# Batch 1's loads of x asked for behind the weights instead of behind a gate, with new instruction tables

## The chip, the cores and the metric

The kernel runs on one core of a Trainium2 chip. The metric is the time of one execution on the device in microseconds. Engines: TensorE (PE in the profile, its weight loads PEld), VectorE (DVE), ScalarE (ACT), GpSimd (POOL) and SyncE (SP), which only asks for transfers. Each engine runs its own instructions in the order in which the program lists them; an instruction that waits holds up all that stand behind it on that engine.

## The reference

```python
# x: 4 x 12480 x 128, inducing: 32 x 128, w_in: 128 x 2048, w_out: 2048 x 128, all float32
def mab(q, kv):                       # softmax attention, scale = 1/sqrt(128)
    s = scale * (q @ kv.transpose(0, 2, 1))
    a = np.exp(s - s.max(-1, keepdims=True))
    a /= a.sum(-1, keepdims=True) + 1e-09
    return a @ kv
h = mab(I, x)                         # 32 inducing rows attend to the 12480 rows of a batch
y = mab(x, h)                         # each row attends to the 32 results
t = y @ w_in
g = t * np.clip(t + 3.0, 0.0, 6.0) / 6.0
out = g @ w_out
```

## The kernel before

A batch (0 to 3) goes through two passes. The rows of a batch are cut into seven *groups*: six of 2048 rows (128 partitions of 16 rows, 1024 KB) and a last one of 192 rows. The groups make 25 *chunks* of up to 512 rows.

**Pass 1** of batch b reads each group once: a load of x into an `xr` buffer (`load_x`, L207, from GpSimd's queue; five such buffers), a cast to bfloat16 in four parts (`k`, L357; buffer `xb`, two of them), transposes on TensorE (`T`, L366) that are copied to `xT` (`x`, L375), scores against the inducing rows (`s`, L381), their exponentials (`a`, L393), the aggregation `hnd` (`g`, L419) and a running sum of the weights (`y`, L432). An `xr` buffer is free again when its group's `g` is done.

**Between the passes**, from the 32 aggregated rows: the sum of the weights (`dred`, `den`, `rD`), `H`, its transpose `HT`, the tables `W` and `Wd` (L492, L498), and `dH`. Because the 32 rows are few, the two layers behind the attention are folded into small coefficient tables. `G` (L517) is the first layer applied to the 32 rows; `hs`, `L`, `lt` and `BD` make the linear table; for the quadratic table, 16 blocks are squared (`dp` L616 and `q` L628 to L631 in batch 0) and multiplied with w_out (`C`, L642), which gives `Cq` (L655).

**Pass 2** of batch b goes chunk by chunk: `bp` (L783) and its exponentials `TF` (L796); the small exponentials `dk` (L762, three buffers, one for each group of chunks) are spread over the partitions by a transfer that SyncE asks for (`d<-dk`, `b_spread`, L771, six buffers `d`); `TD` is the product of both (L807); `op` sums the linear part (`b_lin`, L818) and 16 matmuls with Cq (`b_quad`, L837); VectorE scales the result by r_all (L857) into `os`, which SyncE stores. `ep`, `e`, `sp`, `nf`, `rp` and `r` make r_all.

**The order.** Pass 1 of batch 0, the tables of batch 0 and pass 1 of the first group of batch 1 are the *prologue*; its instructions stand in the list ORDER, token by token, and `first` carries them out. After it comes a loop over all 100 chunks, t = 0 to 99. In step t, chunk t is summed, the `bp` of chunk t + 2 computed, its products one step later, and the spread of chunk t + 6 asked for. All else (the rest of pass 1 of batch 1, then pass 1 and the tables of batches 2 and 3) is put into slots of these steps by the list PLAN: `@2.8 k1.2.3:A` means that in step 2, at place 8 among its places 0 to 28, part 3 of group 2 of batch 1 is cast by ScalarE (A; D is VectorE, P is GpSimd). ORDER and PLAN are written by a planner from costs and due times.

The tokens that the change touches: `dx5`, `dx6` and `dx10` in ORDER ask for groups 5 and 6 of batch 0 and group 0 of batch 1; `dwi` and `dwo` ask for w_in (two transfers) and w_out (four); `held` is a gate and four loads: GpSimd copies one element of the spread of chunk 3, so it waits until that has landed, and then asks for groups 1 to 4 of batch 1. `made` is a gate of the same kind that waits for dH. `wl` and `wo` are the eight and four pieces in which the low part of w_in and the bfloat16 copy of w_out are made; `bk`, `bT`, `bx`, `bs`, `ba`, `bg`, `by` are group 0 of batch 1; `warm` are matmuls whose results nobody reads; `half` is four small VectorE instructions (half_rows). BY_DVE names the blocks whose squares VectorE makes instead of ScalarE.

```python
elif kind == "held":
    gate("seen", S[0][("d", 3)][:, 0:1])
    while held:
        load_x(1, held.pop(0))
```

Of the kernel before, what the change touches and what calls it, by code (L numbers as in the profile page):

```python
# [40 lines left out]
k1.3.2:A g1.1.0 g1.1.1 @5.0 T1.4.0 @5.2 k1.5.1:D @5.3 s1.2 a1.2 lx2.0 @5.4 T1.3.1 @5.7 k1.5.3:A @5.12 y1.2
g1.2.0 k1.5.0:D @5.22 T1.3.0 x1.3.0:A x1.3.1:D x1.4.0:D @6.0 g1.2.1 @6.6 k1.5.2:A @6.8 s1.3 T1.5.0 a1.3 y1.3
k1.6:P T1.6.0 x1.6a @6.24 s1.4 a1.4 x1.5.0:D @7.2 y1.4 lx2.1 @7.3 g1.3.0 g1.3.1 @7.5 sp0.3 T1.5.1 g1.4.0
k2.0.0:P k2.0.3:D @7.8 T1.6.1 x1.6 nf0.3 k2.0.2:D x1.5.1:A @7.22 lx2.2 @7.23 s1.5 a1.5 @8.1 k2.2.2:P @8.3
g1.4.1 @8.21 k2.0.1:D @8.28 s1.6 a1.6 y1.5 y1.6 @9.4 k2.2.1:P @9.5 k2.2.0:P @9.8 T2.0.1 @9.12 dred1 @9.20
T2.0.0 @9.21 lx2.3 @9.22 x2.0.1:A @10.2 k2.1.2:A @10.24 x2.0.0:A @10.28 den1 k2.1.3:A @11.4 g1.5.0 da1 @11.24
g1.5.1 g1.6.0 g1.6.1 rD1 H1 @12.4 s2.0 @12.5 lx2.6 htp1 @12.8 HTb1 @12.12 a2.0 HT1 @12.28 pp0.5 ep0.6 dk0.5
pp0.6 ep0.5 e0.5 lx2.4 HTl1 G1.0 G1.1 G1.2 @13.0 e0.6 @13.3 G1.3 Gc1.0 k2.1.0:A @13.7 g2.0.0 @13.20 Gc1.1
k2.2.3:A g2.0.1 @13.21 hs1 dG1.2 k2.1.1:A @13.22 T2.1.1 x2.1.1:D @13.23 dG1.0 @13.24 sp0.4 @13.28 dk0.6 @14.0
nf0.4 @14.2 sq1.2 @14.6 dG1.3 T2.2.1 x2.2.1:A T2.1.0 sq1.0 k2.3.1:D dG1.1 T2.2.0 x2.2.0:A @14.12 x2.1.0:D Wd1  # L50
L1.0 L1.1 @14.21 Lc1 @14.24 sq1.3 @15.3 lx2.5 @15.5 s2.1 a2.1 @15.6 dG1.4 @15.20 sq1.1 dG1.11 @15.22 k2.3.2:P
y2.0 @16.8 k2.4.0:P @16.28 pp1.0 dk1.0 @17.0 ep1.0 g2.1.0 e1.0 @17.7 lt1 @17.8 sq1.4 sp0.5 nf0.5 k2.3.3:A C1.2
dG1.5 @17.21 C1.0 BD1 @17.23 sq1.5 @18.8 sp0.6 dG1.8 k2.4.3:P @18.20 y2.1 sq1.11 dG1.13 @18.21 C1.4 @19.6
g2.1.1 k2.4.2:A @19.12 sq1.8 @19.23 nf0.6 k2.4.1:P @20.0 sp1.0 @20.1 dG1.12 C1.11 C1.5 @20.6 s2.2 a2.2 @20.24
T2.3.1 sq1.13 @20.28 k2.3.0:D T2.3.0 C1.8 nf1.0 @21.2 dG1.9 g2.2.0 x2.3.1:A @21.5 x2.3.0:D @21.7 sq1.12 @21.8
sq1.9 @21.20 dG1.6 @21.23 dG1.14 @22.12 k2.5.0:P W1 @22.21 C1.3 lx3.0 ep1.2 e1.2 pp1.1 ep1.1 dk1.1 e1.1 pp1.2
@23.0 dk1.2 sq1.6 @23.2 T2.4.1 x2.4.1:D @23.3 dG1.7 C1.13 @23.20 sq1.14 @23.21 dG1.10 @24.12 C1.1 sq1.7 C1.12
@24.20 s2.3 a2.3 dG1.15 k2.5.3:A @24.23 k2.5.1:D C1.6 @25.0 k2.5.2:P @25.2 sp1.2 y2.2 C1.14 g2.2.1 T2.4.0
@25.4 C1.7 g2.3.0 sq1.10 T2.5.0 C1.9 sq1.15 g2.3.1 C1.15 @25.5 x2.4.0:A C1.10 nf1.2 lx3.2 T2.5.1 @25.6 s2.4
x2.5.0:A sp1.1 Cq1 @25.12 nf1.1 x2.5.1:A k2.6:P T2.6.1 @25.28 x2.6 @26.3 a2.4 @26.7 s2.5 @26.22 y2.3 @27.0  # L60
g2.4.0 T2.6.0 g2.4.1 @27.3 a2.5 k3.0.3:P @27.5 x2.6a @27.12 y2.4 @27.24 k3.0.1:P @27.28 s2.6 a2.6 pp1.4 dk1.4
pp1.3 ep1.4 e1.4 y2.5 y2.6 dred2 @28.2 ep1.3 e1.3 @28.3 g2.5.0 g2.5.1 g2.6.0 k3.0.0:A @28.4 den2 rD2 k3.0.2:A
dk1.3 @28.8 da2 @28.22 lx3.1 k3.1.0:D g2.6.1 H2 @29.4 lx3.3 @29.5 T3.0.0 @29.24 htp2 HTb2 @30.6 k3.1.3:A
@30.12 k3.1.1:P @30.23 HT2 HTl2 @31.5 x3.0.0:A lx3.4 @31.8 W2 @31.24 lx3.6 @32.3 T3.1.0 G2.0 G2.1 G2.2 G2.3
@32.4 T3.0.1 x3.1.0:A @32.5 Gc2.0 @32.7 x3.0.1:A k3.1.2:A hs2 @32.8 Gc2.1 dG2.2 @32.20 dG2.9 @33.20 sp1.3
@34.4 k3.2.2:P sq2.2 @34.22 T3.1.1 x3.1.1:D nf1.3 @34.23 k3.3.0:P @35.0 s3.0 a3.0 @35.6 k3.3.1:P @35.12 ep1.6
e1.6 dG2.6 ep1.5 pp1.6 pp1.5 e1.5 dk1.5 @35.21 k3.2.0:D @35.24 k3.2.1:P @36.3 y3.0 @36.7 g3.0.0 sq2.6 @36.20
dk1.6 @36.22 g3.0.1 dG2.0 @36.23 k3.2.3:D k3.3.2:A @36.24 sp1.4 T3.2.0 x3.2.0:A @37.1 k3.3.3:P sp1.5 nf1.5
@37.2 L2.0 L2.1 @37.6 sq2.9 nf1.4 @37.20 dG2.1 @37.21 T3.2.1 x3.2.1:D @37.28 sq2.0 @38.12 dG2.4 @38.20
k3.4.0:A @38.21 k3.4.1:D sq2.1 @39.12 lx3.5 @40.0 dG2.5 @40.2 s3.1 a3.1 C2.2 @40.7 C2.1 @40.20 sq2.4 @40.21  # L70
dG2.3 @40.22 s3.2 a3.2 @40.24 sq2.5 dG2.7 @41.2 T3.3.0 @41.6 T3.3.1 @41.12 x3.3.0:A @41.28 C2.5 @42.5 Lc2
@42.6 C2.6 @42.7 y3.1 @42.8 sq2.7 C2.9 @42.12 dG2.10 @42.22 Wd2 @43.2 x3.3.1:D @43.12 sq2.3 dG2.8 @44.0
k3.4.3:P ep2.0 e2.0 pp2.0 dk2.0 pp2.1 ep2.1 g3.1.0 @44.2 C2.4 e2.1 C2.0 @44.3 dk2.1 @44.4 k3.4.2:P @44.6
k3.5.2:D @44.8 sq2.10 @44.20 g3.1.1 @44.21 dG2.15 @44.22 k3.5.3:D lt2 @44.23 T3.4.1 @44.28 sq2.8 @45.1 T3.4.0
x3.4.0:A sq2.15 BD2 @45.5 x3.4.1:D @45.8 dG2.14 C2.3 dG2.11 g3.2.0 @46.6 sp1.6 @46.24 nf1.6 sq2.14 @47.8 sp2.0
nf2.0 @48.2 C2.8 @48.4 sq2.11 dG2.13 pp2.2 @48.5 ep2.2 e2.2 k3.5.0:D @48.8 dk2.2 @49.0 dG2.12 @49.5 k3.5.1:P
@49.21 s3.4 s3.3 @49.22 C2.10 a3.3 @49.23 sq2.13 y3.2 @50.1 T3.5.1 x3.5.1:D C2.7 @50.3 g3.2.1 @50.4 sq2.12
@50.5 k3.6:A C2.14 C2.15 @50.6 C2.12 C2.11 y3.3 sp2.2 T3.5.0 a3.4 sp2.1 C2.13 Cq2 x3.5.0:A g3.3.0 g3.3.1
g3.4.0 nf2.1 s3.5 a3.5 @50.21 y3.4 nf2.2 @51.20 g3.4.1 g3.5.0 T3.6.1 y3.5 @51.24 x3.6 @52.2 T3.6.0 @52.21
x3.6a @53.8 s3.6 a3.6 y3.6 @54.5 g3.5.1 @54.6 dred3 @55.6 g3.6.0 @55.8 den3 rD3 @55.21 da3 @55.22 g3.6.1 @56.0  # L80
pp2.3 dk2.3 @56.2 H3 ep2.5 pp2.5 e2.5 ep2.3 e2.3 @56.6 htp3 @56.28 HT3 HTb3 HTl3 @57.4 G3.0 G3.1 G3.2 G3.3
Gc3.0 Gc3.1 dG3.1 @57.20 dk2.5 @57.28 dG3.0 pp2.4 dk2.4 hs3 ep2.4 @58.1 ep2.6 @58.28 sp2.3 nf2.3 e2.4 sq3.0
@59.0 dG3.4 @60.3 L3.0 sq3.1 L3.1 @60.4 Lc3 @60.5 C3.0 @60.12 dG3.5 sq3.4 Wd3 @60.21 sp2.4 nf2.4 @61.12 e2.6
@61.22 dG3.7 @62.5 sp2.6 @62.6 sq3.5 @62.21 dG3.3 @63.5 sq3.7 @63.12 nf2.6 @63.20 dG3.9 @63.21 sq3.3 @63.24
dG3.2 @64.6 C3.1 @64.21 pp2.6 pp3.0 dk3.0 ep3.0 e3.0 @65.3 sq3.2 @65.4 dG3.6 @65.22 dk2.6 @65.23 C3.7 W3 sq3.9
@66.3 C3.2 @66.4 C3.3 @66.21 sq3.6 @67.2 dG3.10 @67.6 dG3.15 @67.7 sq3.10 @67.20 sp2.5 @67.23 dG3.8 nf2.5
@68.0 C3.6 @68.5 C3.4 sq3.15 @68.21 dG3.13 @69.6 lt3 @69.8 sq3.8 @70.28 dG3.11 @71.2 C3.15 @71.4 C3.10 @71.7
BD3 @71.21 C3.9 @71.28 sq3.13 @72.5 sq3.11 @72.24 dG3.14 @73.0 pp3.1 dk3.1 @73.3 ep3.1 e3.1 @73.4 dG3.12 @73.6
sp3.0 nf3.0 @73.28 sq3.14 @74.12 C3.13 sq3.12 @74.21 C3.8 @74.23 C3.5 @75.0 C3.11 @75.2 C3.14 C3.12 Cq3 @75.6
sp3.1 pp3.2 ep3.2 dk3.2 e3.2 pp3.4 ep3.4 @75.8 dk3.4 @75.24 nf3.1 @76.3 e3.4 @78.24 sp3.4 nf3.4 @79.4 pp3.3  # L90
# [19 lines left out]


# [1219 lines left out]
```

## Time and profile before

| | |
|---|---|
| median of 3 runs | 292.4 us (291.7 to 293.71) |
| the profiled execution's own time | 292.84 us |
| its span, first to last instruction | 291.1 us |
| granted TensorE clock | 0.995 |
| TensorE busy | 282.1 us, 97% |
| moved by DMA | 66.69 MB, mean 229 GB/s |

Times in the profile are microseconds from the start of the span. A row of instructions reads: start, length, engine, line, operation, what is written from what, and count; in brackets, the idle time before it and what ended that. The rows of windows give for each stretch its length and the busy time of each engine. The prologue lasts to about 43, the loop to about 286.

### The profile page before, as it was taken

The page shows a single profiled execution, that of the slowest core. Times are in us where ns is not written, and L with a number is a line of the kernel's source. Part 1 is how long each engine was busy: PE and PEld are TensorE (multiplying, and loading weights), DVE is VectorE, ACT ScalarE, POOL GpSimd, SP SyncE. Part 2 cuts the span into 40 slices and gives each one's busy share as a digit, 9 for nine tenths or more (in the row PEclk, how much of TensorE's full clock was granted, in tenths as well). Part 3 has the DMA queues.
Part 4 walks back from the last instruction along what each step waited for, and adds up shares of the span by engine and source line. Part 5 has one row for each costly group of instructions (what it writes and reads, how often), then busy time and mean ns, then how long its engine had stood idle before and what let it go on. Part 6 is the DMA issues. An engine that isn't in the chain of part 4 may idle for free.

```text
span 291.1 us, 9807 instructions
## 1 busy us (share of the span) xinstructions
PE 282.1 (97%) x3960; PEld 227.6 (78%) x3971; DVE 231.9 (80%) x495; ACT 227.0 (78%) x412; POOL 130.5 (45%) x250
## 2 busy tenths in 40 slices
...
GB/s 258 428 365 270 104 329 402 231 273 281 285 357 161 245 199 177 336 317 259 295 84 216 305 100 148 214 35 203 160 150 182 172 208 222 146 216 217 229 227 156
DMA packets 25137, 66.69 MB, mean 229 GB/s; under 512 B 3168, under 2 KB 18304, under 8 KB 19072
## 3 DMA queue, kind: packets, MB, share of 16 engines
...
q14 instruction: 17, 0.14, 0.2%
...
## 4 chain that ended last, share of the span: by engine, by line
PE 80%; DMA 11%; DVE 5%; issue 1%; ACT 1%; ACTq 0%; DVEq 0%; POOLq 0%
PE op L837 29%; PE bp L783 13%; PE op L818 8%; PE hnd L419 7%; PE pt L366 5%; DMA xr<-in_x_dram 5%; PE cp L642 5%; DMA out_dram<-os 4%; PE s L381 2%; DMA d<-dk 2%; PE sp L687 2%; PE pp L748 2%; PE ep L667 2%; PE lp L585 1%; PE gp L517 1%
## 5 line engine op out<-in xcount | busy, mean ns | idle before, releaser
L796 ACT ACTIVATE TF<-bp 128x512 bf16<-128x512 f32 (+1 forms) x200 | 115.6, 589 | 32.8 <-PE bp L783 18.9
L837 PE MATMUL op<-Cq,TF 128*128 128x128 bf16 (+1 forms) x784 | 100.3, 221 | 0.1
L837 PE MATMUL op<-Cq,TD 128*128 128x128 bf16 (+1 forms) x784 | 98.6, 219 | 0.0
L857 DVE TENSOR_TENSOR os<-op,r_all 128x512 f32<-128x512 f32 x96 | 65.9, 687 | 20.5 <-PE op L837 18.3
L807 DVE TENSOR_TENSOR TD<-TF,d 128x1024 bf16<-128x1024 bf16 (+1 forms) x100 | 74.8, 748 | 0.2
L837 PEld LDWEIGHTS <-TF 128*128 128x128 bf16 (+1 forms) x784 | 56.1, 98 | 21.2 <-issue 11.0
L783 PE MATMUL bp<-xT,W 128*128 128x512 bf16 (+1 forms) x193 | 72.3, 375 | 0.1
L837 PEld LDWEIGHTS <-TD 128*128 128x128 bf16 (+1 forms) x784 | 60.4, 98 | 0.0
L818 PE MATMUL op<-BD,nf 128*128 128x512 f32 (+1 forms) x100 | 54.7, 547 | 0.0
L357 POOL CAST xb<-xr 128x512 bf16<-128x512 f32 x33 | 25.1, 778 | 29.7 <-DMA xr<-in_x_dram 17.5
L544 POOL COPY gate<-TD 128x1 bf16<-128x1 bf16 x48 | 14.1, 294 | 51.2 <-DVE TD L807 49.2
L547 POOL TENSOR_TENSOR dg<-G 128x256 f32<-128x256 f32 x48 | 35.6, 741 | 0.0
L546 POOL TENSOR_TENSOR dg<-G 128x256 f32<-128x256 f32 x48 | 31.5, 656 | 6.9 <-DVE r_all L736 3.6
L554 ACT ACTIVATE sq<-dg 128x512 bf16<-128x512 f32 x48 | 30.0, 629 | 3.8 <-POOL dg L547 2.1
L419 PE MATMUL hnd<-xr,a 128*32 128x128 f32 x384 | 30.6, 227 | 0.0
L366 PE MATMUL pt<-ident_b,xb 128*128 128x128 bf16 x392 | 29.6, 219 | 1.0 <-DVE xb L357 0.5
L419 PEld LDWEIGHTS hnd<-xr,a 128*32 128x32 f32 x384 | 24.8, 109 | 2.7 <-issue 1.3
L366 PEld LDWEIGHTS <-xb 128*128 128x128 bf16 x392 | 23.2, 98 | 4.6 <-issue 1.6
L726 PE MATMUL rp<-one,nf 128*128 128x4 f32 (+1 forms) x100 | 25.6, 257 | 0.9 <-ACT dk L762 0.9
L375 ACT COPY xT<-pt 128x1024 bf16<-128x1024 bf16 (+1 forms) x24 | 22.4, 950 | 2.8 <-PE pt L366 2.6
L642 PE MATMUL cp<-w_out_b,sq 128*128 128x128 bf16 x256 | 22.4, 220 | 0.1
L726 PEld LDWEIGHTS rp<-one,nf 128*128 128x128 f32 (+1 forms) x100 | 18.9, 189 | 3.7 <-ACT dk L762 1.3
...
## 6 DMA issues: line engine op xcount, KB each, us to landing
xr<-in_x_dram POOLq DMA_DIRECT2D x23, 1024.0 KB, 8.1
out_dram<-os SPq DMA_DIRECT2D x23, 1024.0 KB, 4.6
d<-dk SPq DMA_DIRECT2D x96, 128.0 KB, 4.4
os<-in_x_dram SPq DMA_DIRECT2D x1, 1024.0 KB, 5.7
...
w_out_r<-in_moe_w_out_dram POOLq DMA_DIRECT2D x4, 256.0 KB, 10.8
...
xl<-in_x_dram POOLq DMA_DIRECT2D x4, 96.0 KB, 7.0
```

The source lines that it names most:

```text
L366: nc.tensor.transpose(pt[:, (i - lo) * p : (i - lo + 1) * p], xb[:p, i, :], ident_b[:p, :p])
L419: nc.tensor.matmul(st["hnd"][:M, :C], lhsT=st[("a1", g)][:p, i * M : (i + 1) * M], rhs=xs[(b, g)][:p, i, :], start=(g == 0 and i == 0), st ...
L546: nc.gpsimd.tensor_sub(dg[:, 0], stepped(G2, jb, 0, 1, 0), stepped(G2, jb, 2, 0, 2))
L547: nc.gpsimd.tensor_sub(dg[:, 1], stepped(G2, jb, 1, -1, 0), stepped(G2, jb, 10, 0, 2))
L642: nc.tensor.matmul(st["cp"][:, k * C : (k + 1) * C], lhsT=sq[:, k * P : (k + 1) * P], rhs=w_out_b[:, jc, :], start=(k0 == 0 and k == 0), s ...
L726: nc.tensor.matmul(st["rp"][:p, at : at + S_], lhsT=nf[:R, j * p : (j + 1) * p], rhs=one4[:R, :S_], skip_group_check=True,)
L783: nc.tensor.matmul(st[("bp", c, k)][:, :w], lhsT=st["W"][:, k].rearrange("p m i -> p (m i)"), rhs=st[("xT", g)][:, j * w : (j + 1) * w],)
L796: nc.scalar.activation(st[("x", c)][:, k, :w], bp[:, :w], ACT.Exp, scale=scale)
L807: nc.vector.tensor_mul(u[:, :, :w], t[:, :, :w], d[:, :w].unsqueeze(1).to_broadcast([P, 2, w]))
L818: nc.tensor.matmul(op[:p, : S_ * C], lhsT=st[("nf", g)][:R, j * p : (j + 1) * p], rhs=st["BD"][:R, : S_ * C], start=True, stop=False, skip ...
L837: nc.tensor.matmul(op[:p, s * C : (s + 1) * C], lhsT=T[k][:, s * p : (s + 1) * p], rhs=st["Cq"][:, k, :], start=False, stop=(s == S_ - 1 a ...
L857: nc.vector.tensor_mul(ot[:p, j * S_ : (j + 1) * S_, :], op[:p, : S_ * C].rearrange("p (s c) -> p s c", c=C), r_all[:p, b, c, :S_].unsquee ...
```

## The change

The gate and its four loads go out of ORDER. The loads of groups 1 to 4 of batch 1 become tokens `dx11` to `dx14`, which stand behind the weights' loads (`dwo`) on GpSimd, between its first instructions for batch 1. ORDER and PLAN are both computed anew, for x that is there when the loop begins; BY_DVE has one block less. All other code stays. PLAN holds the same tokens as before in other slots and with other engines for some casts and copies; ORDER holds the same tokens but for the loads, the gate, and 11 warming matmuls instead of 14. ORDER now names the engine of a square (`q7:D`), which `first` doesn't read: BY_DVE decides.

```diff
-BY_DVE = (2, 6, 11)
+BY_DVE = (2, 7)
...
 PLAN = """
-@0.0 ep0.2 k1.1.2:P k1.1.1:A k1.1.3:D e0.2 pp0.4 dk0.4 k1.1.0:P pp0.2 k1.2.0:P ep0.4 e0.4 @0.4 k1.2.2:P @0.5
-dk0.2 @0.12 lx1.6 @0.20 sp0.1 nf0.1 @1.22 T1.1.1 x1.1.1:D lx1.5 T1.1.0 @2.0 k1.2.1:P x1.1.0:A @2.8 k1.2.3:A
-@3.2 pp0.3 dk0.3 ep0.3 e0.3 sp0.2 T1.2.0 nf0.2 k1.3.3:P @3.12 T1.2.1 @3.20 k1.3.1:A @3.22 k1.4.3:D k1.4.0:A
+@0.0 k1.2.0:D ep0.4 k1.2.3:P k1.1.1:D k1.2.2:P k1.1.2:P k1.1.3:A e0.4 pp0.2 dk0.2 pp0.4 dk0.4 @0.3 ep0.2 e0.2
+@0.20 sp0.1 nf0.1 @1.2 k1.1.0:P @1.3 k1.2.1:P @1.12 lx1.5 @1.21 T1.2.1 x1.2.1:D @1.22 T1.1.1 x1.1.1:D T1.1.0
+x1.1.0:A T1.2.0 x1.2.0:D @2.0 lx1.6 @2.4 k1.4.0:A @2.8 k1.4.3:D @2.20 ep0.3 e0.3 pp0.3 dk0.3 @3.2 k1.4.2:P
...
 ORDER = """
-k0.0:A k0.2:D k0.1:A warm3:o T0.1:o T0.0:o xT0.1:A xT0.0:D k1.2 warm3:f s0:f a0 k1.0:D k1.1:P
-T1.1:f z1:D z0:A T1.0:f z3:P xT1.1:D z2:A g0.0 xT1.0:D k2.1:P k2.2 g0.1 k2.0:D s1:f dx5 y0
-T2.1:f a1 dx6 T2.0:o xT2.1:D g1.0 g1.1 k3.0:D k3.2 k3.1:D y1 dx10 T3.0:o xT2.0:A dwi warm2:f
-s2:f T3.1:f dwo k4.0:D k4.1:A xT3.0:D a2 T4.0:f xT3.1:D k4.3:A g2.0 k4.2:A xT4.0:D s3:f T4.1:f
-y2 a3 g2.1 xT4.1:A y3 g3.0 g3.1 s4:o k5.0:D k5.1:A k5.3:D k6:A warm2:o T5.0:o k5.2:D a4 T6:f
-T5.1:f xT5.0:D xT6:A g4.0 xT5.1:D s5.0:f g4.1 y4 a5.0 bk2:P s5.1:f bk0:A s6:f g5.0 bk3:P dred
-a5.1 a6 n5.0 bk1:P n5.1 wi0 g5.1 g6 n6 den bT0:o wl0:P rD H wl1:P bx0:A dall warm1:f htp:f bT1:o
-HT Wd HTb bx1:D wi1 warm1:f pe1:ff HTl dH bs:f dk1 wl4:P pe0:fo W ba wo1:P dp13:o e1 dp6:f by
-bg0 made wl7:P e0 q6 bg1 dk0 wo3:P dp5:f q13 sp0:f wl2:P spread0 dp15:f q5 dp2:f nf0 C6 wl3:P
-C13 q15 q2 dp4:o wo0:P G0:o q4 C5 dp1:f dp0:f C15 q1 wl5:D held bp0.0:f wl6:D dp11:o q0 G1 q11
-G2 TF0.0 C4 wo2:A G3 dp8:f C1 hs dp9:f q8 C0 dp14:f q9 bp0.1:f C11 C8 TF0.1 dp12:o cmax dp3:f C9
-q12 half L0:f q14 L1 q3 dp10:f C2 L dp7:o TD0 q10 lt:o C3 q7 C12 BD C10 C14 C7 bp1.1:f rp0:f Cq
-rp1 bp1.0:f TF1.1 TF1.0 warm2:f r0
+k0.2:D k0.0:D warm4:o T0.1:o k0.1:D xT0.1:A T0.0:o xT0.0:D k1.2 warm3:f s0:f k1.1:D k1.0:P z2:D
+z1:A T1.1:f z0:P a0 T1.0:f xT1.1:D z3:A g0.0 xT1.0:D k2.2 g0.1 k2.0:D s1:f dx5 k2.1:D T2.1:f y0
+a1 dx6 T2.0:o xT2.1:D g1.0 y1 g1.1 k3.2 k3.0:D dx10 k3.1:D xT2.0:A warm1:o T3.1:o dwi T3.0:f
+xT3.1:D s2:f k4.2:A k4.3:D dwo xT3.0:D k4.1:A warm2:f T4.1:f k4.0:D a2 s3:f xT4.1:D T4.0:f a3 y2
+g2.0 xT4.0:A g2.1 y3 g3.0 s4:o g3.1 k5.0:D k5.1:A k6:D dx11 k5.2:A k5.3:D warm1:o T5.0:o a4 T6:f
+T5.1:f xT5.0:D xT6:A g4.0 xT5.1:D s5.0:f g4.1 y4 a5.0 bk3:P s6:f bk2:A s5.1:f g5.0 dx12 dred
+a5.1 n5.0 a6 bk1:A bk0:P g5.1 wi0 half n5.1 dx13 n6 den g6 bT1:o wi1 rD H wl1:D htp:f bT0:o HTb
+HT dx14 bx1:A Wd bx0:D pe1:ff HTl dH bs:f dk1 pe0:fo ba dall W made wo2:P dp7:o e1 dp6:f bg0
+q7:D wo1:P q6:A bg1 wo0:P dk0 dp9:f dp0:f wl3:P by spread0 dp2:f q9:A C7 wl0:P dp8:o q0:A C6
+q2:D C9 q8:A wl2:P dp10:o C0 e0 dp5:f wl5:P C8 q10:A bp0.0:f wl4:D dp15:o G0:f q5:A wl7:D G1
+wl6:P TF0.0 dp11:f C2 wo3:P q15:A dp14:o C10 q11:A G2 G3 q14:A dp12:f dp3:f hs bp0.1:o q12:A C15
+C11 TF0.1 C14 dp1:f q3:A C5 cmax L0:o q1:A dp4:f TD0 L1 q4:A dp13:o sp0:f L q13:A C1 lt:f nf0
+C12 C4 BD C3 C13 bp1.0:f bp1.1:f Cq TF1.0 rp0:o rp1 TF1.1 r0
 """.split()
...
             elif kind == "dx":
-                load_x(*((1, 0) if i == 10 else (0, i)))
+                load_x(i // 10, i % 10)
```

More of the change, by code (lines that the diff above doesn't have):

```diff
@@ L31 @@
 SUMG = 5
-BY_DVE = (2, 6, 11)
+BY_DVE = (2, 7)
 SPLIT = (4, 5)
 PLAN = """
-@0.0 ep0.2 k1.1.2:P k1.1.1:A k1.1.3:D e0.2 pp0.4 dk0.4 k1.1.0:P pp0.2 k1.2.0:P ep0.4 e0.4 @0.4 k1.2.2:P @0.5
-dk0.2 @0.12 lx1.6 @0.20 sp0.1 nf0.1 @1.22 T1.1.1 x1.1.1:D lx1.5 T1.1.0 @2.0 k1.2.1:P x1.1.0:A @2.8 k1.2.3:A
-@3.2 pp0.3 dk0.3 ep0.3 e0.3 sp0.2 T1.2.0 nf0.2 k1.3.3:P @3.12 T1.2.1 @3.20 k1.3.1:A @3.22 k1.4.3:D k1.4.0:A
-@4.2 x1.2.1:D s1.1 @4.3 k1.4.2:P a1.1 k1.3.0:A @4.4 T1.4.1 x1.4.1:D @4.5 x1.2.0:D @4.6 k1.4.1:A @4.24 y1.1
@@ L41 @@
[L41 to L90, printed above, removed]
@@ L91 @@
-dk3.3 ep3.3 @79.28 e3.3 @80.6 sp3.2 nf3.2 @82.3 sp3.3 @83.5 nf3.3 @85.4 ep3.5 e3.5 ep3.6 e3.6 pp3.5 pp3.6
-@86.6 dk3.6 @87.8 sp3.5 nf3.5 @88.24 sp3.6 @89.0 dk3.5 @93.5 nf3.6
+@0.0 k1.2.0:D ep0.4 k1.2.3:P k1.1.1:D k1.2.2:P k1.1.2:P k1.1.3:A e0.4 pp0.2 dk0.2 pp0.4 dk0.4 @0.3 ep0.2 e0.2
+@0.20 sp0.1 nf0.1 @1.2 k1.1.0:P @1.3 k1.2.1:P @1.12 lx1.5 @1.21 T1.2.1 x1.2.1:D @1.22 T1.1.1 x1.1.1:D T1.1.0
+x1.1.0:A T1.2.0 x1.2.0:D @2.0 lx1.6 @2.4 k1.4.0:A @2.8 k1.4.3:D @2.20 ep0.3 e0.3 pp0.3 dk0.3 @3.2 k1.4.2:P
@@ new lines @@
+@3.3 s1.1 @3.5 k1.3.3:D @3.8 k1.3.0:D a1.1 @3.20 k1.4.1:P T1.4.0 @3.23 x1.4.0:D T1.4.1 s1.2 @3.24 x1.4.1:A
+@4.0 a1.2 @4.1 k1.3.1:P @4.4 k1.5.0:P @4.6 g1.1.0 T1.3.0 x1.3.0:A g1.1.1 g1.2.0 @4.20 k1.3.2:P T1.3.1 @4.28
+k1.5.1:D y1.1 y1.2 @5.3 s1.4 a1.4 k1.6:P @5.6 sp0.2 @5.22 g1.2.1 x1.3.1:D @5.23 k1.5.3:A @5.28 T1.6.1 @6.3
+lx2.0 @6.4 nf0.2 k1.5.2:A @6.5 s1.3 a1.3 y1.3 @6.8 T1.5.0 x1.5.0:A @6.21 x1.6 @6.24 g1.3.0 @7.0 g1.3.1 sp0.3
+@7.2 T1.6.0 T1.5.1 @7.4 nf0.3 g1.4.0 g1.4.1 @7.6 x1.6a lx2.2 k2.0.2:P s1.6 @7.12 lx2.1 x1.5.1:A @7.21 k2.0.3:D
@@ new lines @@
+@7.23 k2.0.1:P @7.24 k2.0.0:A @8.6 k2.1.0:P @8.8 y1.4 s1.5 a1.5 lx2.4 @8.21 T2.0.1 k2.1.1:P T2.0.0 a1.6
+x2.0.1:A @8.24 k2.2.2:A @8.28 y1.5 @9.0 y1.6 k2.1.2:P @9.2 g1.5.0 x2.0.0:A @9.8 dred1 @10.8 g1.5.1 @10.12
+lx2.3 den1 rD1 @10.20 k2.2.0:A k2.2.1:A @10.21 g1.6.0 g1.6.1 da1 @10.28 H1 s2.0 a2.0 @11.8 htp1 HT1 Wd1 @11.20
+HTb1 @12.0 W1 HTl1 @12.28 pp0.5 dk0.5 ep0.5 ep0.6 e0.6 k2.1.3:D pp0.6 dk0.6 e0.5 k2.2.3:A @13.0 G1.0 G1.1 G1.2
+G1.3 Gc1.0 Gc1.1 @13.2 hs1 @13.24 lx2.6 T2.1.1 x2.1.1:A @13.28 sp0.4 dG1.0 @14.5 T2.2.0 x2.2.0:A @14.6 dG1.2
@@ new lines @@
+@14.8 y2.0 @14.21 sq1.0 dG1.3 g2.0.0 nf0.4 @15.3 T2.1.0 x2.1.0:D k2.3.3:A @15.5 L1.0 @15.7 sq1.2 @15.12 g2.0.1
+sq1.3 @15.20 dG1.1 T2.2.1 x2.2.1:D @15.22 L1.1 Lc1 @16.0 dG1.4 @16.3 C1.0 k2.3.2:A @16.4 lx2.5 k2.4.0:P s2.1
+sq1.1 k2.4.1:D a2.1 @16.5 sq1.4 dG1.11 @16.6 lt1 @16.8 BD1 @16.12 k2.4.2:P @17.2 y2.1 @17.23 C1.3 @17.28 ep1.0
+e1.0 @18.2 pp1.0 dk1.0 dG1.8 k2.3.1:P g2.1.0 @18.3 sp0.5 @18.6 sp1.0 @18.8 nf0.5 @18.12 nf1.0 sq1.11 @18.21
+s2.2 @18.28 k2.3.0:A dG1.5 @19.0 C1.4 @19.3 a2.2 @19.4 sq1.8 @19.6 C1.2 @19.21 g2.1.1 @19.22 sp0.6 nf0.6
@@ new lines @@
+@19.23 sq1.5 @20.1 dG1.12 dG1.9 @20.3 lx3.0 @20.4 C1.8 @20.12 sq1.12 @20.21 dG1.13 T2.3.1 x2.3.1:D @21.3 sq1.9
+@21.7 T2.3.0 x2.3.0:D @21.12 k2.5.0:A @21.21 dG1.6 @21.23 C1.9 sq1.13 @22.2 y2.2 k2.4.3:P dG1.14 @22.21 pp1.2
+dk1.2 pp1.1 dk1.1 ep1.2 e1.2 ep1.1 C1.1 @22.24 e1.1 @23.0 C1.11 sq1.6 @23.8 sq1.14 dG1.7 T2.4.1 x2.4.1:D
+@23.12 C1.5 @23.24 k2.5.3:D dG1.10 @24.2 sq1.7 @24.8 k2.5.1:A @24.20 s2.3 dG1.15 g2.2.0 C1.7 @24.21 a2.3 C1.13
+@24.22 sp1.2 C1.6 C1.12 @24.23 T2.4.0 g2.2.1 @25.0 nf1.2 C1.14 @25.1 g2.3.0 T2.5.0 lx3.2 sq1.10 C1.10 sq1.15
@@ new lines @@
+C1.15 x2.5.0:A @25.2 k2.6:P T2.6.0 @25.3 x2.4.0:D s2.4 a2.4 @25.4 x2.6a Cq1 @25.5 k2.5.2:P @25.6 T2.5.1 g2.3.1
+@25.12 y2.3 y2.4 k3.0.2:D @25.24 x2.5.1:A @25.28 sp1.1 nf1.1 @26.22 g2.4.0 g2.4.1 @26.23 s2.5 @26.28 k3.0.0:A
+a2.5 @27.0 T2.6.1 x2.6 @27.20 y2.5 @27.24 k3.0.1:P @27.28 s2.6 a2.6 lx3.1 g2.5.0 y2.6 dred2 k3.0.3:A @28.0
+ep1.3 e1.3 @28.3 pp1.3 pp1.4 dk1.4 ep1.4 e1.4 dk1.3 g2.5.1 @28.4 k3.1.0:A @28.12 k3.1.3:D @28.20 den2 rD2
+g2.6.0 g2.6.1 @28.23 da2 @29.0 H2 @29.2 T3.0.1 @29.28 htp2 x3.0.1:D @30.4 k3.1.1:A HTb2 HT2 HTl2 @30.12 W2
```

28 lines of the change are left out of this document (added).

## The prediction

> **What bounds the kernel now.** I read the head of the page and the chain by engine first, to see which engine is the limit, then the busy time by stage, to see where that engine rests.
>
> ```profile
> span 291.1 us, 9807 instructions
> PE 282.1 (97%) x3960; PEld 227.6 (78%) x3971; DVE 231.9 (80%) x495; ACT 227.0 (78%) x412; POOL 130.5 (45%) x250
> PE 80%; DMA 11%; DVE 5%; issue 1%; ACT 1%; ACTq 0%; DVEq 0%; POOLq 0%
> ```
> ```profile
> core 0: us, PE busy (x) PEld busy (x) DVE busy (x) ACT busy (x) POOL busy (x), PEclk, DMA share, GB/s
> 0.00:44.00 44.00, 40.73 (x578) 29.47 (x585) 30.74 (x64) 32.91 (x58) 25.75 (x62) 1.00 0.94 293
> 44.00:285.00 241.00, 239.90 (x3371) 197.15 (x3374) 199.28 (x422) 194.04 (x356) 104.71 (x188) 1.00 0.68 220
> 285.00:291.00 6.00, 1.49 (x19) 1.00 (x16) 1.86 (x11) 0.00 (x0) 0.00 (x0) 0.77 0.34 118
> ```
>
> TensorE is busy for 97% of the span and carries 80% of the chain. The loop (44 to 285) leaves it idle for 1.10 us of 241. The change issues the same matmuls in the loop, so whatever it does for x can bring back about 1.1 us there at most. The 3.27 us of idle time before 44 is the only other place, and 4.5 us at the end are the last stores, which the change doesn't touch.
>
> Where is the loop's one idle stretch? The chain in order of time, then TensorE's own row:
>
> ```profile
> 43.50 6.29 DMA d<-dk
> ...
> 51.37 0.61 ACT dk L762
> 52.02 0.27 PE rp L726
> ```
> ```profile
> 52.02 0.27 PE L726 MATMUL rp<-one,nf 128*128 128x4 f32 x1 [0.86 <-ACT dk L762]
> ```
>
> A broadcast of d asked for at 43.50 lands late. It reads a dk buffer, there are three of these, and ScalarE can't write the next dk until it has landed; TensorE waits 0.86 us behind that. A late d is unusual, so I looked at what else the DMA engines carried (columns: window, length, TensorE busy, clock, DMA share, GB/s), and at single transfers in two of the windows (KB each, median us to landing):
>
> ```profile
> 25.00:31.00 6.00, 5.98 (x91) 1.00 1.11 156
> 31.00:37.00 6.00, 5.75 (x93) 1.00 0.56 134
> 37.00:43.30 6.30, 6.30 (x79) 1.00 0.97 349
> 43.30:50.00 6.70, 6.70 (x85) 1.00 1.09 404
> ```
> ```profile
> d<-dk SPq DMA_DIRECT2D x6, 128.0 KB, 2.8
> ```
> ```profile
> q0 software_dynamic: 292, 2.18, 96.0%
> q1 hardware_dynamic: 9, 0.01, 0.9%
> xr<-in_x_dram POOLq DMA_DIRECT2D x3, 1024.0 KB, 9.5
> d<-dk SPq DMA_DIRECT2D x1, 128.0 KB, 7.2
> ```
>
> From 31 to 37 the engines move 134 GB/s and six d take 2.8 us each. From 37 to 50 four loads of batch 1 fill them (349 and 404 GB/s), and a d takes 7.2. These loads start there because of the gate:
>
> ```profile
> 20.55 0.81 POOL L246 DMA_DIRECT2D w_out_r<-in_moe_w_out_dram  x1 [1.75 <-DMA xr<-in_x_dram]
> ...
> 33.05 0.60 POOL L259 CAST w_out_b<-w_out_r 128x512 bf16<-128x512 f32 x1
> 35.93 0.19 POOL L873 COPY seen<-d 128x1 bf16<-128x1 bf16 x1 [2.28 <-DMA d<-dk]
> 36.17 2.20 POOL L207 DMA_DIRECT2D xr<-in_x_dram  x4
> 41.42 1.18 POOL L357 CAST xb<-xr 128x512 bf16<-128x512 f32 x2 [3.04 <-DMA xr<-in_x_dram]
> ```
>
> So the trade of the change is plain: the four loads leave the window of the loop's d (37 to 50) and enter that of the first six d (31 to 37).
>
> **The change, part by part.** The sum is made against the profiled execution's own time, 292.84 us (span 291.1, 1.74 around it), which is 0.44 above the median of the three runs.
>
> *The gate goes, the loads come earlier.* The gate's copy (0.19) and its wait (2.28) leave GpSimd, where only these loads stood behind it: nothing on the path. The four issues cost 2.20 us of GpSimd as before. Now they stand behind the last w_out_r issue (20.55). That issue itself waited 1.75 us, for a load asked for eight GpSimd transfers earlier: with this, each of the four can go only when the transfer eight before it has landed, and when the aggregation has released its x buffer. The loads eight before are the tail of x, batch 1's group 0 and the two halves of w_in; the fourth thus goes at about 27, and GpSimd has nothing to do for a table until dH is there (below), so this wait holds up nobody for long. Data flows behind the weights:
>
> ```profile
> DMA to landing us min/median/max: 9.1/10.8/10.9
> ```
>
> This is w_out_r; 20.55 + 9.1 gives 29.7. Four times 1024 KB are 4.19 MB, at 404 GB/s 10.4 us: x is there at about 40 with nothing else in the way, at about 42 with the six d in between (0.79 MB more). Before, the fourth was asked for at 38, and the last three took 9.5 us in the median: 47. So "there when the loop begins" holds within a few us.
>
> *What it buys.* At 43.5 the loads are over; the d of that time takes 2.8 us instead of 7.2, and the wait of 0.86 goes. What is late next there? The row of the loop leaves 1.10 - 0.86 = 0.24 us of idle time: nothing that a profile can name. Bounds: 0 (the new table waits elsewhere) to 1.1. I take **-0.86**.
>
> *What it may cost: the first six d.*
>
> ```profile
> 31.15 18.47 SPq L771 DMA_DIRECT2D d<-dk  x10
> ...
> 39.87 9.75 SPq L771 DMA_DIRECT2D d<-dk  x4
> ```
> ```profile
> 28.62 0.42 DVE L505 TENSOR_TENSOR dH<-HT 128x256 bf16<-128x256 f32 x1
> ...
> 31.84 0.68 DVE L697 CUSTOM_DVE_ANT_0 nf<-e,sp 128x512 fp32r<-128x512 f32 x1
> ...
> 36.06 0.69 DVE L570 TENSOR_SCALAR r<-gp 128x512 f32<-128x512 f32 x1
> ...
> 38.96 0.28 DVE L596 TENSOR_SCALAR L<-lp 32x128 f32<-32x128 f32 x1 [0.26 <-PE lp L585]
> 39.17 0.67 DVE L807 TENSOR_TENSOR TD<-TF,d 128x1024 bf16<-128x1024 bf16 x1
> 40.05 0.69 DVE L606 TENSOR_TENSOR BD<-lt,one_f 128x512 fp32r<-128x512 f32 x1 [0.21 <-PE lt L601]
> 41.27 0.56 DVE L655 TENSOR_SCALAR Cq<-cp 128x384 bf16<-128x384 f32 x1 [0.53 <-PE cp L642]
> ```
>
> The first d is asked for at 31.15. With the loads beside it I give it the 7.2 us of the one d that stood behind them: 38.4 instead of 34. The new ORDER puts TD0 (which reads it) ahead of L, nf0 and BD on VectorE; before, TD0 came after L and nf0 long before. So VectorE can start Cq, which opens the loop, at the landing + 0.67 + 0.28 + 0.68 + 0.69 = +2.32. 38.4 gives 40.7; the old start is 41.27. **Hidden, with 0.6 us to spare.** The point from which it decides is a landing at 38.95. The d for chunks 1 to 5 have until 42.8 and later.
>
> The Trainium skill (DMA: Bandwidth & Descriptors, section "Queues, rings and completion order") says that each DMA engine goes round-robin between the queues that have work, a packet at a time. By that rule the first d would get every second packet from the start, and land at some 36, with 3 us to spare. The row speaks against relying on it: between 37 and 43.3, with a d asked for at 39.87, the queue of d moved 9 packets while that of the loads moved 292. I go by the row.
>
> *The new ORDER.* The same instructions, but for the three warming matmuls fewer in it (14 before, 11 now), of which the last two filled the wait for Cq: nothing. One square less on VectorE and one more on ScalarE, one cast of w_out less on ScalarE: ScalarE has 21 instructions from dk1 to the last square in both. Their rows:
>
> ```profile
> 28.56 0.61 ACT L762 ACTIVATE dk<-pp 128x512 bf16<-128x512 f32 x1
> ...
> 37.63 2.65 ACT L631 ACTIVATE sq<-dpm 128x512 bf16<-128x512 f32 x5
> ```
> ```profile
> L631 ACT ACTIVATE sq<-dpm 128x512 bf16<-128x512 f32 x13 | 7.0, 612 | 0.7 <-PE dpm L616 0.5
> L255 POOL TENSOR_TENSOR w_in_l<-w_in_r,w_in_b 128x256 bf16<-128x256 f32 x4 | 2.8, 708 | 1.4 <-ACT w_in_b L250 1.4
> L259 POOL CAST w_out_b<-w_out_r 128x512 bf16<-128x512 f32 x3 | 2.0, 672 | 0.0
> ```
>
> ScalarE's squares end at 40.28 and set Cq; in front of them it rested 0.7 us, which a better order could win. The other way: GpSimd had four of its nine weight pieces behind it when it passed "made"; now all nine come after it, 5 x 0.71 + 4 x 0.67 = 6.2 us from about 29.3 (dH is there at 29.04), so 35.5 instead of 33.65, 1.9 later. The last of them feeds the C of blocks 12 to 15, whose squares come last anyway, and the eighth, at 34.8, feeds the last G, whose sum VectorE began to read at 36.06: hidden by about 1 us, and 0.9 us worse if that cover is gone. half_rows (four small VectorE instructions) moves into a wait of VectorE ahead of H: nothing on the path. So **-0.2**, bounds -0.7 and +0.9.
>
> *The new PLAN.* The same tokens in other slots; which engine casts and copies changes. In batch 1, GpSimd gets 11 casts instead of 8, ScalarE 4 instead of 9, VectorE 6 instead of 4. TensorE's work is the same to the matmul. Bounds: 0 to +2.6, three waits of the size of the one that goes (0.86); 0 is the value, since the old table has but one.
>
> Sum: 292.84 - 0.86 - 0.2 = 291.8 by the profiled execution, 291.3 by the median; I say **291.4**.
>
> **Rivals.**
>
> *A, nothing to measure.* The loop's idle time was 1.10 us, and another late buffer takes the place of the d. For it: every table has some, and x was hidden already but for this one place, as GpSimd alone waited for it (3.04). Against: the wait has one clear cause. 292.4, between 292.0 and 293.0.
>
> *B, slower: the first d sits behind the loads.* Its place is TD0 at the loop's opening, its condition a landing after 38.95. If the queue of d gets nothing until the loads end, as from 39.87 to 43, that is 29.7 + 10.4 = 40.1, and 1.5 us more for the d itself: 41.6, Cq at 43.9 instead of 41.27, +2.6, less the 0.86 that still goes: +1.8. At the 349 GB/s of the window 37 to 43.3 the loads end at 41.7 and it is +3.4. Between the two, 292.4 + 2.6 = 295.0. For it: the nine packets. Against: they did begin to move before the loads had ended.
>
> *C, faster: the prologue gains too.* With ScalarE's 0.7 and another 1.0 of the 3.27 us that TensorE rests before 44, the loop opens 1.7 earlier: 292.4 - 0.86 - 1.7 = 289.8. For it: squares wait for dpm. Against: ScalarE's 21 instructions are the same.
>
> *D, slower by the tables:* several new waits in the PLAN, at the bound of 2.6 above: 292.4 + 2.6 = 295.0, or a bit over it.
>
> **How the numbers follow.** My forecast has 0.45 (its own range 290.4 to 292.3), A 0.15, B 0.15, C 0.14, D 0.11. A change of 1%, 2.9 us, is about what a measurement of this kernel can tell from none. Faster by more needs C and a little beyond it: 0.10. Slower by more takes the upper part of B and D and what lies beyond: 0.21. Within 1%: 0.69. The range reaches from C (289.7) to a little over B and D, 295.6.
>
> **What would show it.** Right: the four loads issued between 21 and 28; no d over 4 us after 43; no 0.86 us wait at the fourth chunk; loop begun within 1 us of 43.2; TensorE idle under 0.6 us in the loop. Wrong: TD0 waiting for d (B); waits of TensorE for xb, xT or TF in the loop's first ten chunks (D); a d as late as before with x gone (then x was never its cause).

## The result, and the profile after

The changed kernel takes 295.21 us (median of 12 runs, 294.12 to 296.51), the kernel before 291.97 beside it: the ratio is 1.0094, 95% interval 1.0071 to 1.0117. The forecast was 291.4, a gain; the change is slower by 0.9% instead, at the upper end of the range given. The two profiled executions, 295.47 and 292.84, are 2.63 apart, less than the medians, because the old one was slower than its median.

Head of the page, then the busy time by stage, both of the changed kernel:

```profile
span 293.7 us, 9805 instructions
PE 281.6 (96%) x3968; PEld 227.7 (78%) x3968; DVE 233.7 (80%) x503; ACT 220.9 (75%) x406; POOL 125.2 (43%) x246
PE 77%; DMA 10%; DVE 5%; ACT 4%; issue 2%; POOL 0%; ACTq 0%; DVEq 0%; POOLq 0%
```
```profile
0.00:44.00 44.00, 39.25 (x564) 29.05 (x565) 29.52 (x65) 29.66 (x52) 26.71 (x64) 1.00 1.12 360
44.00:285.00 241.00, 238.25 (x3362) 195.37 (x3354) 199.89 (x425) 190.17 (x353) 98.50 (x182) 1.00 0.64 204
```

TensorE rests more in both stages: 4.75 us before 44 (3.27 in the old kernel) and 2.75 from 44 to 285 (1.10). Its work is the same (busy for 281.6 us, before 282.1). Chunk 0's linear product starts at 44.64 instead of 43.20, chunk 99's at 288.03 instead of 285.37: 1.44 us are lost before the loop and 1.22 in it, 2.66 together, which is the growth of the span (291.1 to 293.7). Each part has one large wait. A small one stands beside them in the loop, 0.40 us at 100.43 ahead of `s` (L381): every profile with the new tables has it, none with the old, and its cause stays open.

**The opening.** GpSimd's own rows: the four loads go out at 21 to 27.

```profile
21.21 0.55 POOL L207 DMA_DIRECT2D xr<-in_x_dram  x1
...
23.20 0.54 POOL L207 DMA_DIRECT2D xr<-in_x_dram  x1
...
25.21 0.53 POOL L207 DMA_DIRECT2D xr<-in_x_dram  x1 [0.85 <-DVE dacc L434]
26.61 0.53 POOL L207 DMA_DIRECT2D xr<-in_x_dram  x1 [0.86 <-PE hnd L419]
```

The six d are asked for from 31.59 on. The DMA queues from 31 to 37 (packets, MB, share) and the median landing of these d:

```profile
q0 software_dynamic: 323, 2.37, 102.2%
q1 hardware_dynamic: 68, 0.07, 4.3%
...
d<-dk SPq DMA_DIRECT2D x6, 128.0 KB, 8.0
```

They take 8.0 us instead of 2.8. The chain in order of time and VectorE's and TensorE's rows show who pays:

```profile
31.59 9.04 DMA d<-dk
...
40.73 0.69 DVE TD L807
```
```profile
40.73 0.69 DVE L807 TENSOR_TENSOR TD<-TF,d 128x1024 bf16<-128x1024 bf16 x1 [2.33 <-DMA d<-dk]
41.34 0.27 DVE L596 TENSOR_SCALAR L<-lp 32x128 f32<-32x128 f32 x1
41.54 0.67 DVE L697 CUSTOM_DVE_ANT_0 nf<-e,sp 128x512 fp32r<-128x512 f32 x1
...
42.19 0.69 DVE L606 TENSOR_TENSOR BD<-lt,one_f 128x512 fp32r<-128x512 f32 x1
43.19 0.56 DVE L655 TENSOR_SCALAR Cq<-cp 128x384 bf16<-128x384 f32 x1 [0.31 <-PE cp L642]
```
```profile
41.66 0.48 PE L601 MATMUL lt<-L,sel 32*128 32x128 f32 x2 [1.67 <-DVE L L596]
```

TD0 stands first in VectorE's queue and waits 2.33 us for d. L, nf0 and BD stand behind it; TensorE waits 1.67 us for L with `lt`, and four of the C products stand behind `lt`. Cq begins at 43.19 instead of 41.27.

**The loop.** The old wait at the fourth chunk is gone: with the loads over, the d asked for from 43.3 to 50 land in 2.5 us.

```profile
d<-dk SPq DMA_DIRECT2D x2, 128.0 KB, 2.5
```

But a longer one stands at 154, in the chain and in TensorE's and ScalarE's rows:

```profile
144.35 9.27 DMA d<-dk
...
153.78 0.33 ACT dk L762
```
```profile
154.15 0.38 PE L783 MATMUL bp<-xT,W 128*128 128x512 bf16 x1 [2.11 <-ACT dk L762]
```
```profile
153.78 0.32 ACT L762 ACTIVATE dk<-pp 32x192 bf16<-32x192 f32 x1 [3.28 <-DMA d<-dk]
```

It is the same wait as the old one at 52: the next dk can't be written until a d that reads its buffer has landed. What is in the way here, by SyncE's and GpSimd's rows:

```profile
143.11 0.34 SPq L867 DMA_DIRECT2D out_dram<-os  x1
143.50 5.30 SPq L771 DMA_DIRECT2D d<-dk  x4
```
```profile
142.55 0.57 POOL L207 DMA_DIRECT2D xr<-in_x_dram  x1
```

A store of 1024 KB and a load of x, both asked for in the microsecond before the first of these d. The d follow the store in SyncE's queue: it lands at 152.98, 9.87 us after it was asked for, and they from 153.27 on. In the old kernel the store is there too (at 141.38, and it took 5.72), but no load is asked for between 131.32 and 157.74. The load is lx3.3 (group 3 of batch 3), which the new PLAN has in step 32 instead of 29.

### The profile page after: what moved, and what is told of

Same layout as the page of the kernel before. It is cut to its first block, busy times and chain, and to the rows that moved or that the text cites. A ratio compares the mean times of both kernels' runs of the same rounds, so it can differ in the third digit from the quotient of the medians.

```text
span 293.7 us, 9805 instructions
## 1 busy us (share of the span) xinstructions
PE 281.6 (96%) x3968; PEld 227.7 (78%) x3968; DVE 233.7 (80%) x503; ACT 220.9 (75%) x406; POOL 125.2 (43%) x246
## 3 DMA queue, kind: packets, MB, share of 16 engines
q1 hardware_dynamic: 18880, 39.40, 41.6%
## 4 chain that ended last, share of the span: by engine, by line
PE 77%; DMA 10%; DVE 5%; ACT 4%; issue 2%; POOL 0%; ACTq 0%; DVEq 0%; POOLq 0%
PE op L837 29%; PE bp L783 13%; PE op L818 8%; DMA d<-dk 6%; PE pt L366 5%; PE hnd L419 5%; PE cp L642 4%; DMA xr<-in_x_dram 3%; PE s L381 3%; PE sp L687 2%; PE pp L748 2%; PE ep L667 1%; DVE dacc L434 1%; DVE xT L375 1%; PE gp L517 1%
## 5 line engine op out<-in xcount | busy, mean ns | idle before, releaser
L807 DVE TENSOR_TENSOR TD<-TF,d 128x1024 bf16<-128x1024 bf16 (+1 forms) x100 | 73.0, 730 | 5.6 <-ACT TF L796 2.7
L783 PE MATMUL bp<-xT,W 128*128 128x512 bf16 (+1 forms) x200 | 74.8, 375 | 2.2 <-ACT dk L762 2.1
L544 POOL COPY gate<-TD 128x1 bf16<-128x1 bf16 x48 | 13.1, 273 | 62.8 <-DVE TD L807 59.8
L547 POOL TENSOR_TENSOR dg<-G 128x256 f32<-128x256 f32 x48 | 38.6, 805 | 0.0
L357 POOL CAST xb<-xr 128x512 bf16<-128x512 f32 x30 | 18.9, 644 | 31.5 <-PE pt L366 19.0
L546 POOL TENSOR_TENSOR dg<-G 128x256 f32<-128x256 f32 x48 | 30.3, 631 | 4.0 <-ACT sq L554 1.5
L375 DVE COPY xT<-pt 128x1024 bf16<-128x1024 bf16 (+1 forms) x36 | 21.3, 602 | 8.0 <-PE pt L366 7.7
L375 ACT COPY xT<-pt 128x1024 bf16<-128x1024 bf16 (+1 forms) x20 | 18.6, 937 | 9.9 <-PE pt L366 9.6
L783 PEld LDWEIGHTS <-W 128*128 128x128 bf16 x200 | 19.4, 97 | 3.4 <-issue 2.5
```

What stands on the lines that cost most here:

```text
L375: eng(S[b][("xT", g)][:, lo * p : hi * p], pt[:, : (hi - lo) * p])
L546: nc.gpsimd.tensor_sub(dg[:, 0], stepped(G2, jb, 0, 1, 0), stepped(G2, jb, 2, 0, 2))
L547: nc.gpsimd.tensor_sub(dg[:, 1], stepped(G2, jb, 1, -1, 0), stepped(G2, jb, 10, 0, 2))
L783: nc.tensor.matmul(st[("bp", c, k)][:, :w], lhsT=st["W"][:, k].rearrange("p m i -> p (m i)"), rhs=st[("xT", g)][:, j * w : (j + 1) * w],)
L807: nc.vector.tensor_mul(u[:, :, :w], t[:, :, :w], d[:, :w].unsqueeze(1).to_broadcast([P, 2, w]))
```

## The experiments

Theory X: all that is lost is lost by d transfers that stand behind loads of x, at two places. Its rivals: T, the new tables are slower by themselves; S, the loads in question are not what makes d late.

### e1: the new tables with the gate

```diff
-k6:D dx11 k5.2:A ... g5.0 dx12 dred ... n5.1 dx13 n6 ... HT dx14 bx1:A ... wo3:P q15:A
+k6:D k5.2:A ... g5.0 dred ... n5.1 n6 ... HT bx1:A ... wo3:P held q15:A
```

> New tables, but the four loads behind the gate again (asked for once the spread of chunk 3 has landed, at the end of GpSimd's prologue). Theory X (the first six d stand behind the loads of x): they land in about 3 us again instead of 8, TD0 waits for nothing, Cq begins at about 41.3 instead of 43.2. The loop's first casts, which the tables put at its very start, then find no x and cost 1 to 2.5 us on VectorE, and the wait at 154 (2.1) stays: 294 to 295.5 us in all. Rival T (the new ORDER is slower by itself): Cq begins at 43 as in the changed kernel, whatever d does, and the time is 296 to 298.

Measured: 295.56 us (10 runs, 294.51 to 297.29), ratio 1.0072 (1.0028 to 1.0116). VectorE's rows:

```profile
37.81 0.68 DVE L807 TENSOR_TENSOR TD<-TF,d 128x1024 bf16<-128x1024 bf16 x1
...
40.95 0.56 DVE L655 TENSOR_SCALAR Cq<-cp 128x384 bf16<-128x384 f32 x1 [0.31 <-PE cp L642]
...
44.23 1.18 DVE L357 CAST xb<-xr 128x512 bf16<-128x512 f32 x2 [2.35 <-DMA xr<-in_x_dram]
45.33 1.09 DVE L807 TENSOR_TENSOR TD<-TF,d 128x1024 bf16<-128x1024 bf16 x1
```

TD0 waits for nothing, and Cq begins at 40.95: the new ORDER is not slower by itself, T falls for the opening. But PLAN's first casts find no x, VectorE waits 2.35 us for it ahead of chunk 1's product, and TensorE 1.11. The new tables need the early loads and suffer from them; with the gate they are no better. The wait at 154 stays (2.05 at 153.4). The time came out a little above the range expected; the last section shows one more cost in this profile.

### e2: the old tables with the early loads

```diff
-k6:A warm2:o ... g5.0 bk3:P ... n5.1 wi0 ... HT Wd ... wl5:D held bp0.0:f
+k6:A dx11 warm2:o ... g5.0 dx12 bk3:P ... n5.1 dx13 wi0 ... HT dx14 Wd ... wl5:D bp0.0:f
```

> Old tables, but the four loads asked for behind the weights and no gate. Theory X: the first six d take about 8 us here too; TD0 comes behind L and nf0 in this ORDER, so Cq slips by 0.8 to 1 us only, and the wait of 0.86 at the fourth chunk goes: 291.7 to 292.5 us, the same as before. Rival T: the early loads alone cost nothing and the wait goes: 291.0 us.

Measured: 291.51 us (10 runs, 291.14 to 292.72), ratio 0.9959 (0.993 to 0.9988). The d are late (first the DMA issues of 31 to 37), and VectorE doesn't care:

```profile
d<-dk SPq DMA_DIRECT2D x6, 128.0 KB, 11.0
```
```profile
38.70 0.28 DVE L596 TENSOR_SCALAR L<-lp 32x128 f32<-32x128 f32 x1
38.91 0.67 DVE L807 TENSOR_TENSOR TD<-TF,d 128x1024 bf16<-128x1024 bf16 x1
39.79 0.69 DVE L606 TENSOR_TENSOR BD<-lt,one_f 128x512 fp32r<-128x512 f32 x1 [0.21 <-PE lt L601]
41.01 0.56 DVE L655 TENSOR_SCALAR Cq<-cp 128x384 bf16<-128x384 f32 x1 [0.53 <-PE cp L642]
```
```profile
44.00:285.00 241.00, 240.70 (x3381) 197.89 (x3385) 201.08 (x429) 193.77 (x355) 101.29 (x183) 1.00 0.65 209
```

The six take 11.0 us in the median, more than in the changed kernel, but the first is there within 8, before the old ORDER comes to TD0. Cq even begins 0.26 earlier than before; the slip that was expected did not come. (The 0.26 is no gain to read: the repeat below has Cq at 41.30.) TensorE rests 0.30 us in the loop instead of 1.10. So in this profile the early loads alone bring what the forecast's main term said, 0.8 us in the loop. That is what rival T of this experiment said; the time lies between its 291.0 and the 291.7 at which the range of theory X begins.

### e2 once more

> The kernel of e2 (old tables, early loads, no gate) on the same chip as e6 and e7, with more rounds: if the early loads alone are a gain, it is again faster than the kernel before by 0.2 to 0.6%, 291.0 to 291.8 us here; if that was the chip of that day, the interval holds 1.

Measured: 291.62 us (12 runs, 291.51 to 294.63) beside 292.42, ratio 0.9992 (0.9964 to 1.0019). The median is 0.8 us lower again, but the interval holds 1: two of the twelve runs took 294.5 and 294.6, at a lower mean clock (0.991 where the others have 0.994 to 0.999). The trace agrees with e2's: TensorE rests 0.13 us in the loop. That e2 beats the kernel before is thus likely, not settled.

### e3: TD0 moved behind Cq

```diff
-q1:A dp4:f TD0 L1 ... bp1.1:f Cq TF1.0
+q1:A dp4:f L1 ... bp1.1:f Cq TD0 TF1.0
```

> The changed kernel with one token moved: TD0, which waits for the first d, stands behind Cq on VectorE instead of ahead of L. Theory X: d is as late as in the changed kernel (8 us), but L, nf0, BD and Cq no longer wait for it: Cq at 41.3 to 41.6, TD0 right behind it, loop begun 1.4 to 1.9 us earlier, 293.4 to 293.8 us. Rival T: another engine holds the opening of the loop too, and less than 0.5 us comes back: 294.8 or more.

Measured: 293.87 us (10 runs, 293.12 to 296.84), ratio 1.0051 (1.0011 to 1.0091). Rows of VectorE:

```profile
41.57 0.56 DVE L655 TENSOR_SCALAR Cq<-cp 128x384 bf16<-128x384 f32 x1 [0.31 <-PE cp L642]
...
42.30 0.69 DVE L807 TENSOR_TENSOR TD<-TF,d 128x1024 bf16<-128x1024 bf16 x1
```

The d are still late (6.9 us in the median), nobody waits for them, Cq begins 1.62 earlier, and the loop 1.61. The cost of the late d was where TD0 stood in VectorE's queue. It is these rows that show it: the interval overlaps that of the changed kernel (from 1.0071), so the times alone would not. The time is 0.07 us above the range expected; the wait in the middle of the loop stays (1.93 at 152.35).

### e4: lx3.3 from step 32 to step 29

```diff
-H2 @29.2 T3.0.1 @29.28 htp2 ... @32.28 lx3.3 @33.1
+H2 @29.2 T3.0.1 @29.4 lx3.3 @29.28 htp2 ... @33.1
```

> The changed kernel with one token of PLAN moved: the load of group 3 of batch 3 (lx3.3) from step 32 to step 29, so that it is over when the d of chunk 15 of batch 1 is asked for, whose landing the last dk of batch 1 waits for. Theory X: the wait of 2.1 us at 154 goes, the opening stays as it is: 293.0 to 293.4 us. Rival S (the store of 1024 KB ahead of that d in the same queue makes it late, not the load): the wait stays over 1.5 us, 294.8 or more.

Measured: 292.87 us (10 runs, 292.15 to 293.45), ratio 1.0006 (0.9979 to 1.0032). GpSimd asks for this load at 125.32, and TensorE's busy time in the loop is

```profile
44.00:285.00 241.00, 240.03 (x3377) 197.65 (x3384) 201.47 (x431) 190.64 (x354) 98.05 (x182) 1.00 0.65 208
```

that is 0.97 us of rest instead of 2.75; the wait at 154 is gone. S falls: the store alone does not make that d late enough to be waited for. Both have a part in it, though: with the load beside it the store took 9.87 us, without it 4.20 (asked for at 142.15), and the d behind it in its queue land right after it. The time is 0.13 us below the range expected, because the opening did not stay as it was: in this profile the first d took 8.09 us and landed at 39.67, and the loop began at 43.68 instead of 44.64. What the moved load alone brings is read from the loop, from chunk 0's linear product to chunk 99's: 241.10 us instead of 243.39.

### e6: two loads early, two behind the gate, with e4's move

```diff
-held = [1, 2, 3, 4]
+held = [3, 4]
-n5.1 dx13 n6 ... HT dx14 bx1:A ... wo3:P q15:A
+n5.1 n6 ... HT bx1:A ... wo3:P held q15:A
```

> The changed kernel with only groups 1 and 2 of batch 1 loaded behind the weights, groups 3 and 4 behind the gate again, and lx3.3 moved as in e4. Theory X (a d waits for what is queued ahead of it): half the bytes, so the loads ahead end 5 us earlier, at about 34.5, and the first d lands after 4 to 5.5 us instead of 8; TD0 waits under 0.3 us, Cq at 40.9 to 41.4, and with the wait at 154 gone too: 290.8 to 291.6 us. Rival S (any load beside them makes d as late as four do): the first d takes 7 to 8 us again, Cq at 42.5 or later, 292.7 or more.

Measured: 291.9 us (12 runs, 291.02 to 292.26), ratio 0.9977 (0.9959 to 0.9994). The DMA issues from 31 to 37 and VectorE's TD0:

```profile
d<-dk SPq DMA_DIRECT2D x6, 128.0 KB, 3.9
```
```profile
38.65 0.68 DVE L807 TENSOR_TENSOR TD<-TF,d 128x1024 bf16<-128x1024 bf16 x1
```

Half the loads ahead, and d takes 3.9 us instead of 8.0 (none ahead, e1: 3.0). So it is the amount in flight that counts. What follows may count too: in e2 two more loads were asked for at 36.03 and 36.58, behind the six d, and the last four of these took 10.6 to 12.0 us; no run separates that. Cq begins at 41.78, 0.4 later than expected, but not because of TD0: it comes 9.85 us after the first d was asked for, as in e1 (31.93 to 41.78, 31.10 to 40.95), and why that was 0.8 later here stays open. The time is 0.3 us above the range expected. This version is faster than the kernel before, by 0.2% (interval without 1).

### e7: e3 and e4 together

> The moves of e3 (TD0 behind Cq) and e4 (lx3.3 in step 29) together in the changed kernel, all four loads early. Theory X: the two costs are separate and all that the changed kernel lost; both come back: 291.0 to 291.8 us, not slower than the kernel before. Rival T (the new tables cost something beside): 292.5 or more.

Measured: 291.94 us (12 runs, 291.32 to 292.72), ratio 0.9987 (0.9973 to 1.0001). Against the changed kernel's 1.0094 that is all of its loss: two tokens moved, TD0 and lx3.3. The two gains are separate by place; their sum by the ratios (0.43% and 0.88%) is 0.24% more than what came together, and e4's share has some of the opening in it. The time is 0.14 us above the range expected. TensorE rests 0.97 us in the loop here as in e4, 0.30 in e2 (0.40 of the difference is the small wait near 100): the new PLAN has nothing over the old one.

## Why the prediction was wrong, point by point

*The wait of 0.86 goes*: right, in the changed kernel and, alone, in e2. The loads went out at 21 to 27 as worked out, and the fourth landed at 40.46 (40 to 42 said).

*The first six d: "hidden, with 0.6 us to spare"*: **this step failed, by its size.** The rule was right to 0.24: Cq starts 2.32 after the landing, and a landing after 38.95 decides. The landing was put at 38.4, from one d that had taken 7.2 beside such loads. It was asked for at 31.59 (31.15 said) and took 9.04: 40.63, which gives 42.95 by the rule; measured, 43.19. So a term put at nothing was +1.92 for Cq and +1.44 for the loop's opening. That was rival B, with +2.6 for Cq; its 1.5 us for the d behind the last load did not come, the first d landed 0.17 after that load.

The old profile had more than the one row. The d asked for at 43.50, whose wait was the forecast's main term, took 7.7, which leaves 0.1 us to spare and not 0.6. And the nine packets were misread. They were not of the d asked for at 39.87, but of the one before it, which landed at 38.34. From 38.4 to 43.3 the queue of d doesn't show at all in the old kernel:

```profile
q0 software_dynamic: 276, 2.05, 104.9%
```

That d's queue stood still for 3.4 us, then, which spoke for B; what was said against B (they did begin to move before the loads had ended) doesn't follow from that row. The four profiles of the new ORDER with all four loads early show the spread: the first d took 9.04 (changed kernel), 7.44 (e3), 8.09 (e4) and 7.59 (e7) and landed at 40.63, 39.16, 39.67 and 39.39, always past 38.95, though by little in three of them. Nor is a late d unusual, though the forecast called it so: 17 of the old kernel's 100 took over 6 us. What matters is whether an engine waits for it.

*The new ORDER at -0.2*: its nine weight pieces on GpSimd ended at 35.9 (35.5 said), and VectorE read G's sum at 36.38 instead of 36.06. With d out of the way (e3, e7) Cq begins at 41.6, 0.3 later than before, but the loop begins at 43.03 and 43.09 instead of 43.20. So the term is -0.1 to -0.2 at the loop's opening, as said, though two profiles of one kernel (e2) differ by 0.3 there.

*The new PLAN at 0*: **the second step that failed.** Its value was 0 within 0 to 2.6, and one wait of 2.11 us came, beside the small one of 0.40. The forecast looked for new waits at casts and copies, engine by engine, and never asked where PLAN's moved loads fall beside the d of the loop, though that collision was its own main term at 43.5. What was needed was in the diff: lx3.3 in step 32, and the dk of the last group in step 36 with three buffers.

The sum by the trace: -0.86 and +2.11 in the loop, +1.44 at its opening, 2.69 against 2.66 found. That it closes so well is partly luck: the 0.40 is not in it, and TensorE's busy time is 0.5 less in the new profile. It is luck, too, that the 295.0 of B and D lies near the 295.21 measured: B's part came smaller, and the rest came from a wait that B doesn't have and that D looked for elsewhere. Of the signs named beforehand, B's came (TD0 waiting for d); D's, waits for xb, xT or TF in the first ten chunks, did not.
